# Moving four weight sums and one seventh product in the late schedule of a fused attention and feed-forward kernel

## The chip, the cores and the metric

The kernel runs on one core of a Trainium2 chip. A core has a matrix engine (TensorE, PE in the profile, with weight loads shown apart as PEld), a vector engine (VectorE, DVE), a scalar engine (ScalarE, ACT), a general engine (GpSimd, POOL) and a queue for transfers (SyncE, SP). The metric is the device time of one execution in microseconds. Four executions of the kernel before took 423.79, 424.94, 425.1 and 426.74 us; the median is 425.02 us.

## What is computed

Eight batches of twelve heads with 448 tokens and 64 columns per head go through an attention with normalised queries and keys. The result, 3584 tokens by 768 columns, goes through two weight matrices with a leaky rectifier between them.

```python
q_n, k_n = (rmsnorm(q, g_q), rmsnorm(k, g_k))
scores = scale * np.matmul(q_n, k_n.transpose(0, 1, 3, 2))
attn = softmax(scores)                    # over the last axis
x = (attn @ v), heads side by side        # 3584 x 768
h = x @ w_in                              # 768 x 2048
g = np.maximum(0.01 * h, h)
out = g @ w_out                           # 2048 x 768
```

The softmax and the last lines are abridged; inputs and output are float32.

## The kernel before

**Units.** Attention runs in units `u` of four heads: three units to a batch, 24 in all (`NU`). In each unit the loop over `d` = 0 to 3 issues the scores of one key step (`d` = 0) or two (`STEPS`), then the exponentials (`ex`, line 214) on ACT. With `d` = 0 come three more things: the shift of the exponent for this unit (`shift_max` and `shift_mm`: a maximum, a product `dg`, two small matmuls on PE at line 244, a maximum, and a small operation, four on DVE), and for the unit before it the product with the values (`pv_slot`, line 341) and the sums of the exponentials (`zcol`, line 283). After the shift, ACT copies the old unit's product (`x32`, line 295) before it computes the new exponential; DVE adds up the sums (line 300); ACT makes the reciprocals through logarithm and exponential (lines 305 and 306); SP spreads them by DMA (`rz`) and POOL multiplies (line 321).

**The queue of feed-forward work.** `push(b)` puts the feed-forward items of batch `b` into a queue, and `fill(u, d, jobs)` issues some after each group of scores, by a running account of the items' costs (1.13, 0.575 and 1.31). After each item it issues one of the step's `jobs` (normalisation of a later unit, weight sums and the like). An item is a group of matmuls on PE. What follows it on DVE and ACT is put on a list (`later`), and issued when the next item begins (`flush`). Every engine works through its instructions in the order in which they were issued.

**The late batches.** The last two batches, 6 and 7, use Strassen's scheme (seven products instead of eight) for the first weight matrix. An item is written `(n, s)`: product `n` of strip `s`, where a strip is two of the eight blocks of 128 columns in each half of the 2048. A product is six matmuls of 128x224 (line 565). In batch 6 only strips 2 and 3 are done in this way: its list is `LATE_HALF`, and an "M" in it is one plain block with six matmuls of 128x448 (`moe1`, line 363). Eight M items cover strips 0 and 1. In batch 7 all four strips are (`LATE_ALL`). Batch 6 is pushed at unit 21, `d` = 3, and issued in units 22 and 23; batch 7 follows after the last unit.

In `late1` the products work like this:

- `(1, s)` fills a bank and is copied to `u`; `(2, s)` is added to `u`, and ACT turns that into one quarter of the strip's output (line 575).
- `(7, s)` fills a second bank and is copied to `v` (line 613).
- `(6, s)` accumulates onto the bank of `(1, s)`; an addition (line 578) writes that plus `v` into the bank of `(7, s)`.
- `(5, s)` accumulates further onto the first bank; an addition puts that plus `v` into `v`, and ACT activates it.
- `(4, s)` accumulates onto the second bank, and `(3, s)` onto the first; ACT activates each from its bank.

So `(5, s)` may only start when the addition of `(6, s)` has read the bank, and `(3, s)` only after the addition of `(5, s)`. Four banks serve all of this: `hold` takes them, and `drop` puts one back at the end of a list, from whose head the next is taken. M items draw from the same list.

**Weight sums.** Four products need sums of weight blocks: `win_sum(n, x)` with `n` = 1 to 4 (line 534), each one DVE operation over 128x1536. `x` = 1 serves strips 2 and 3, and is needed by batch 6; `x` = 0 serves strips 0 and 1, which only batch 7 needs. Sum 3 is written over a block of the weights themselves, which the M items read. The four sums with `x` = 0 are jobs of unit 23: two at `d` = 0 and two at `d` = 2.

**After the late products** of batch 6 come the output items: `moe2` (line 404), in four parts for one tile, then `seven` (line 445) for two more tiles. The first part reads blocks 0 to 7 of `gt`, the activated values; the sums `s1` to `s4` of `gt` (lines 426 to 435) are made on DVE behind the four parts. `zsum_slot`, `zinv` and `xmul` finish unit 23, and then batch 7's items run to the end.

Of the kernel before, what the change touches and what calls it, by code (L numbers as in the profile page):

```python
# [18 lines left out]
def kernel(  # L19
# [18 lines left out]
    NU = B * NQ  # L38
# [7 lines left out]
    raws = ctx.enter_context(tc.tile_pool(name="raws", bufs=3))  # L46
    prep_p = ctx.enter_context(tc.tile_pool(name="prep", bufs=2))
# [75 lines left out]
    def load_v(u):  # L123
# [8 lines left out]
        n16=([P, 2, NS, 2, D], FP16, 1), qkT=([P, 2, NS, P], FP16, 3))  # L132
# [226 lines left out]
    def moe1(b, ft):  # L359
        xt = xts[b]  # L360
        hps = aux([P, 512], FP32, "hps")
        for kt in range(KT):
            nc.tensor.matmul(hps[:, 0:S], win16[:, kt // 2, kt % 2, ts(ft, P)], xt[:, kt // 2, kt % 2],  # L363
                             start=(kt == 0), stop=(kt == KT - 1))
        prelu(b, gt[:, ft, 64 * (b % 2):64 * (b % 2) + S], hps[:, 0:S])
        drop(hps)
# [22 lines left out]
    def flush():  # L389
        while pend:  # L390
            pend.pop(0)()
# [45 lines left out]
    def later(fn, *args):  # L437
        pend.append(lambda: fn(*args))
# [81 lines left out]
    def win_b(i, j, f0, n):  # L520
        c = DF // 2 * i + P * f0
        return win_f[:, HK * j:HK * j + HK, c:c + P * n]

    def win_sum(n, x, tile_=None, eng=nc.vector):
        if tile_ is None:
            ws[n, x] = win_b(1, 0, 4 * x, 4)
        else:
            pool, tag, bufs = tile_
            ws[n, x] = pool.tile([P, HK, 512], FP16, tag=tag, bufs=bufs, name="ws")
        a, b = {1: (lambda: (win_b(1, 0, 4 * x, 4), win_b(1, 1, 4 * x, 4))),  # L530
                2: (lambda: (ws[1, x], win_b(0, 0, 4 * x, 4))),
                3: (lambda: (win_b(0, 0, 4 * x, 4), win_b(1, 0, 4 * x, 4))),
                4: (lambda: (win_b(0, 1, 4 * x, 4), ws[2, x]))}[n]()
        eng.tensor_tensor(ws[n, x], a, b, op=ALU.add if n == 1 else ALU.subtract)
# [18 lines left out]
    def late1(b, tail, after):  # L553
# [45 lines left out]
        def item(n, s):  # L599
# [29 lines left out]
            for fn in after.get((n, s), ()):  # L629
# [3 lines left out]

    LATE_ALL = ((1, 0), (2, 0), (7, 0), (1, 1), (6, 0), (7, 1), (1, 2), (5, 0), (4, 0), (6, 1), (3, 0), (2, 1), (7, 2), (5, 1),
                (4, 1), (6, 2), (3, 1), (1, 3), (7, 3), (5, 2), (4, 2), (6, 3), (3, 2), (2, 2), (5, 3), (4, 3), (2, 3), (3, 3))
    LATE_HALF = ("M", "M", "M", "M", "M", "M", (1, 2), (2, 2), (7, 2), "M", (6, 2), "M", (5, 2), (4, 2), (1, 3), (3, 2), (2, 3), (7, 3),
                 (6, 3), (5, 3), (4, 3), (3, 3))

    queue = []

    def also(fn, *more):
        def both():
            fn()
            for m in more:
                m()
        return both

    def push(b):
        pair, odd = divmod(b, 2)
        fast = b > 0  # L650
        order = [f // 2 + HF * (f % 2) for f in range(FT)] if odd else range(FT)
        items = [(1.13, lambda ft=ft: (flush(), moe1(b, ft))) for ft in order]
        half = [(slice(0, 4)), (slice(4, 8))]
        late = b >= LATE
        after = {}
        if late:
            if odd:
                tt = (3, 4)
                for ns, f in (((1, 3), s1), ((4, 2), s2), ((3, 2), s3), ((5, 3), s4)):
                    after[ns] = [lambda f=f: f(tt, half[0])]  # L660
                after[3, 3] = [lambda f=f: f(tt, half[1]) for f in (s1, s2)]
            item = late1(b, odd, after)
            fts = [0, 8, 1, 9, 2, 10, 3, 11]
            items = []
            for w in (LATE_ALL if odd else LATE_HALF):
                if w == "M":
                    items.append((1.13, lambda ft=fts.pop(0): (flush(), moe1(b, ft))))
                else:
                    items.append((0.575, lambda w=w: item(*w)))
        if odd:  # L670
            tt, tn = (3, 4), (5, 6)
            items += [(1.31, fn) for fn in seven(pair, tt, tn)]
            for n, x, fs in ((len(items) - 7, 1, (s3, s4)),) if late else ((8, 0, (s1, s2)), (10, 0, (s3, s4)), (FT - 1, 1, (s1, s2)), (FT, 1, (s3, s4))):
                c, fn = items[n]
                items[n] = (c, also(fn, *[lambda f=f, x=x: later(f, tt, half[x]) for f in fs]))
            items += [(1.31, fn) for fn in seven(pair, tn, None, b == B - 1)]
        else:
            tiles = (2,) if fast else (0, 1, 2)
            std = [lambda t=t, h=h, p=p: moe2(pair, t, h, p) for t in tiles for h in range(2) for p in range(2)]
            if fast:  # L680
                tt = (0, 1)
                std[0] = also(std[0], lambda: later(s1, tt))
                std[1] = also(std[1], lambda: later(s2, tt))
                std[2] = also(std[2], lambda: later(s3, tt), lambda: later(s4, tt))
                std += seven(pair, tt)
            items += [(1.31, fn) for fn in std]
        queue.extend(items)
# [53 lines left out]
    with tc.manual_schedule():  # L741
# [182 lines left out]
        for u in range(3, NU):  # L924
            for d in range(4):
                if d > 0 or u > 3:
                    qk(u, STEPS[d])
                    if d == 0:
                        shift_max(u)
                        if narrow(u - 1):  # L930
                            pv_slot(u - 1)
                            zcol(u - 1)
                            shift_mm(u)
                            pv_out(u - 1)
                            zcol_sum(u - 1)
                        else:
                            zsum_slot(u - 1)
                            pv(u - 1)
                            shift_mm(u)
                            zinv(u - 1)  # L940
                    ex(u)
                jobs = []

                def job(fn, *args):
                    jobs.append(lambda: fn(*args))

                if d == 0:
                    if u == 3:
                        prep_norm(4)
                        gate(4)  # L950
                    elif narrow(u - 1):
                        job(zcol_inv, u - 1)
                    else:
                        xmul(u - 1)
                    if u + 4 < NU:
                        job(load, u + 4)
                    if u + 3 < NU:
                        load_v(u + 3)
                    if u < 6:
                        prep_sqp(u + 3)  # L960
                if d == 1 and narrow(u - 1) and not 5 <= u < 8:
                    xmul_pool(u - 1)
                if fed(u, d) and u > 3:
                    push(u // NQ - 1)
                if (u, d) in ((3, 1), (4, 0)):
                    for ti in range(2):
                        prep_tr(u + 1, ti, VV)
                if d == 1 and 5 <= u < NU - 1:
                    job(prep_g, u + 1)
                if u + 2 < NU:  # L970
                    if d == 1:
                        for ti in range(2):
                            job(prep_ssq, u + 2, ALL, (ti,))
                    if d == 2:
                        job(prep_rinv, u + 2)
                        for ti in range(2):
                            job(prep_norm, u + 2, ALL, (ti,))
                        if u > 3:
                            job(prep_trd, u + 2)
                if d == 1 and 4 <= u < 8:  # L980
                    job(weight_sum, u - 4, 0)
                if d == 0 and 5 <= u < 9:
                    job(weight_sum, u - 5, 1)
                if d == 2 and 5 <= u < 8:
                    job(xmul_sb, u - 1)
                if u == NU - 2 and d == 0:
                    for n, tile_ in ((1, (raws, "rq", 3)), (2, (raws, "rk", 3)), (3, None), (4, (prep_p, "sq", 3))):
                        job(win_sum, n, 1, tile_)
                    for n in (3, 1, 2, 4):
                        job(x_sum, LATE, n)  # L990
                if u == NU - 1 and d in (0, 2):
                    for n, tile_ in (((1, (raws, "rq", 3)), (3, None)), ((2, (raws, "rk", 3)), (4, (prep_p, "n16", 1))))[d // 2]:
                        job(win_sum, n, 0, tile_)
                if d == 3 and 6 <= u < NU - 3:
                    for ti in range(2):
                        job(prep_sq, u + 3, ALL, (ti,))
                fill(u, d, jobs)
# [39 lines left out]
```

## Time and profile before

| | |
|---|---|
| median of four executions | 425.02 us (423.79 to 426.74) |
| profiled execution, time | 425.1 us |
| profiled execution, span from first to last instruction | 423.3 us |
| mean granted clock of TensorE | 0.996 of full speed |
| PE busy | 404.4 us, 96% of the span |
| ACT busy | 305.0 us, 72% |
| DVE busy | 280.0 us, 66% |
| POOL busy | 83.4 us, 20% |

Line numbers (L565 and the like) are those of the kernel before. "Busy" on PE includes matmuls that run at a reduced clock. The row of granted clock gives the clock in 40 equal slices of 10.6 us, in tenths, 9 being 90% or more. In a timeline, a row is a run of like instructions: start, duration of the whole run, engine, line, operation, what is written and read, shapes, how many, and in brackets how long the engine was idle before it and what released it. Matmuls overlap, so the time that one group takes from PE is read from start to start.

The last 80 us of the span hold the stages that the change touches: unit 22 begins near 337 us, unit 23 near 356 us, batch 7's products run from 384 to 400 us, and its output items from there to the end.

### The profile page before, as it was taken

The page shows a single profiled execution, that of the slowest core. Times are in us where ns is not written, and L with a number is a line of the kernel's source. Part 1 is how long each engine was busy: PE and PEld are TensorE (multiplying, and loading weights), DVE is VectorE, ACT ScalarE, POOL GpSimd, SP SyncE. Part 2 cuts the span into 40 slices and gives each one's busy share as a digit, 9 for nine tenths or more (in the row PEclk, how much of TensorE's full clock was granted, in tenths as well). Part 3 has the DMA queues.
Part 4 walks back from the last instruction along what each step waited for, and adds up shares of the span by engine and source line. Part 5 has one row for each costly group of instructions (what it writes and reads, how often), then busy time and mean ns, then how long its engine had stood idle before and what let it go on. Part 6 is the DMA issues. An engine that isn't in the chain of part 4 may idle for free.

```text
span 423.3 us, 9152 instructions
## 1 busy us (share of the span) xinstructions
PE 404.4 (96%) x3731; PEld 218.6 (52%) x3731; DVE 280.0 (66%) x459; ACT 305.0 (72%) x474; POOL 83.4 (20%) x75
## 2 busy tenths in 40 slices
PE   7787999989999999999999999999999999899996
PEld 7454454444445544454445544454445556458953
DVE  5888685888569736675458736576459775547762
ACT  5999877768887599877887689877887576553600
POOL 1867432200010220210210210210220110200000
PEclk9999999999999999999999999999999999899999
DMA  8999997888664996678564895677532650212023
GB/s 269 218 248 243 242 251 116 210 152 201 157 152 83 205 255 93 155 182 173 145 149 82 218 210 117 161 182 170 154 67 45 132 149 2 45 39 75 2 52 98
DMA packets 71950, 62.39 MB, mean 147 GB/s; under 512 B 36325, under 2 KB 67045, under 8 KB 71909
## 3 DMA queue, kind: packets, MB, share of 16 engines
q1 hardware_dynamic: 61312, 49.62, 46.5%
q0 software_dynamic: 10272, 11.80, 17.6%
q8 instruction: 29, 0.48, 0.5%
q10 hardware_dynamic: 324, 0.39, 0.3%
q14 instruction: 13, 0.10, 0.1%
HBM read 45.61 MB, written 11.01 MB: 134 GB/s over the span
## 4 chain that ended last, share of the span: by engine, by line
PE 83%; DVE 8%; ACT 7%; issue 1%; DVEq 0%
PE hps L363 27%; PE sT L195 8%; PE sT L341 6%; PE ma L445 5%; PE md L445 5%; PE mc L445 5%; PE bank L565 5%; PE bank L445 5%; ACT et L214 5%; PE zc L283 3%; PE op L404 3%; PE mb L445 3%; DVE n L167 2%; PE warm L739 2%; PE sT L445 2%; PE bank L404 1%
## 5 line engine op out<-in xcount | busy, mean ns | idle before, releaser
L214 ACT ACTIVATE et<-sT,eb 128x896 f16<-128x896 f32 x166 | 159.6, 1010 | 18.4 <-PE sT L195 16.7
L363 PE MATMUL hps<-xt,win 128*128 128x448 f16 x600 | 121.0, 353 | 0.4 <-DVE xt L350 0.2
L363 PEld LDWEIGHTS <-win 128*128 128x128 f16 x612 | 56.8, 98 | 58.5 <-issue 10.0
L321 POOL TENSOR_TENSOR xt<-x,rz 128x896 f16<-128x896 f32 x16 | 33.7, 2107 | 143.8 <-DMA rz<-zs 96.9
L167 DVE TENSOR_TENSOR n<-rq,rinv 128x896 f16<-128x896 f32 (+2 forms) x25 | 26.7, 1072 | 51.6 <-ACT rinv L161 48.5
L357 ACT ACTIVATE gt<-hps 128x448 f16<-128x448 f32 x100 | 52.4, 549 | 5.6 <-PE hps L363 5.3
L195 PE MATMUL sT<-qkT 64*64 64x448 f16 x664 | 52.2, 363 | 4.4 <-ACT et L214 3.0
L155 DVE TENSOR_REDUCE ssq<-sq 128x14 f32<-128x896 f32 (+2 forms) x49 | 50.4, 1059 | 0.6 <-ACT sq L144 0.6
L445 PEld LDWEIGHTS <-sa 128*128 128x128 f16 x352 | 32.8, 98 | 26.3 <-issue 6.1
L295 ACT COPY x<-sT 128x896 f32<-128x896 f32 x19 | 17.2, 906 | 36.6 <-DVE sT L245 36.6
L124 POOL DMA_DIRECT2D vt<-in_v_dram x24 | 18.2, 759 | 115.5 <-PE sT L341 108.0
L195 PEld LDWEIGHTS <-qkT 64*64 64x64 f16 x672 | 15.4, 104 | 37.7 <-issue 34.2
L445 PEld LDWEIGHTS <-gt 128*128 128x128 f16 x264 | 25.2, 98 | 18.7 <-issue 2.1
L341 PE MATMUL sT<-et,vt 64*64 64x448 f16 x532 | 28.5, 349 | 0.3
L404 PE MATMUL op<-wout,gt 128*128 128x384 f16 x160 | 28.4, 327 | 0.0
L232 DVE TENSOR_REDUCE sT<-sT 128x1 f32<-128x896 f32 x22 | 24.1, 1094 | 4.9 <-PE sT L195 4.7
L341 PEld LDWEIGHTS <-vt 64*64 64x64 f16 x672 | 20.7, 107 | 11.3 <-issue 1.7
L167 DVE TENSOR_TENSOR n<-rk,rinv 128x896 f16<-128x896 f32 (+2 forms) x26 | 26.1, 1011 | 0.0
L404 PEld LDWEIGHTS <-gt 128*128 128x128 f16 x192 | 17.8, 98 | 13.8 <-issue 3.1
L445 PE MATMUL ma<-wout,gt 128*128 128x384 f16 x128 | 23.5, 326 | 0.0
L426 DVE TENSOR_TENSOR sa<-gt 128x512 f16<-128x512 f16 (+1 forms) x15 | 8.1, 543 | 15.9 <-ACT gt L357 12.1
L144 ACT ACTIVATE sq<-rq 128x896 f32<-128x896 f32 (+2 forms) x18 | 16.3, 913 | 1.3 <-DMA rq<-in_q_dram 1.3
(136 smaller groups left out, 525.5 us busy)
## 6 DMA issues: line engine op xcount, KB each, us to landing
rq<-in_q_dram SPq DMA_DIRECT2D x24, 448.0 KB, 4.4
rk<-in_k_dram SPq DMA_DIRECT2D x24, 448.0 KB, 5.6
out_dram<-ost SPq DMA_DIRECT2D x52, 192.0 KB, 2.9
rz<-zs SPq DMA_DIRECT2D x76, 112.0 KB, 2.3
vt<-in_v_dram POOLq DMA_DIRECT2D x24, 224.0 KB, 5.7
win<-in_moe_w_in_dram POOLq DMA_DIRECT2D x8, 384.0 KB, 14.2
wout<-in_moe_w_out_dram POOLq DMA_DIRECT2D x2, 1536.0 KB, 28.9
out_dram<-ost SPq DMA_DIRECT2D x4, 96.0 KB, 2.1
```

Of the source, the lines that this page charges most:

```text
L155: nc.vector.tensor_reduce(buf(u, "ssq")[:, ti, :, c[0]:c[1]], buf(u, f"sq{ti}")[:, :, c[0]:c[1]], axis=AXL.X, op=ALU.add)
L167: nc.vector.tensor_tensor(buf(u, "n16")[:, ti, c[0]:c[1]].rearrange("p s a d -> p a s d"), src[:, :, c[0]:c[1]], buf(u, "rinv")[:, ti, :, ...
L195: nc.tensor.matmul(banks[a][64 * r:64 * r + 64, 0:S].rearrange("p (t x) -> p t x", t=NS), kT(u, r, a, t), qT(u, r, a), start=True, stop=True)
L214: nc.scalar.activation(s["et"][:, t], sT[:, :, 0:S], AF.Exp, bias=s["eb"], scale=1.0)
L232: nc.vector.tensor_reduce(s["spare"][:, 511:512], sT[:, :, 0:S], axis=AXL.XY, op=ALU.max)
L321: eng.tensor_tensor(xts[b][:, g], s["x32"], s["rz"], op=ALU.mult)
L341: nc.tensor.matmul(s["pv"][r][64 * a:64 * a + 64, 0:S], vts[u % NV][64 * r:64 * r + 64, a, t], s["et"][64 * r:64 * r + 64, t, a], start=(t ...
L357: nc.scalar.activation(dst, src, AF.Prelu, bias=0.0, scale=1.0, alpha=0.01)
L363: nc.tensor.matmul(hps[:, 0:S], win16[:, kt // 2, kt % 2, ts(ft, P)], xt[:, kt // 2, kt % 2], start=(kt == 0), stop=(kt == KT - 1))
L404: nc.tensor.matmul(op2[:, 0:HC], gt[:, ft, ds(col(t), P)], wout16[:, ft, ds(HC * half, HC)], start=(ft == 0), stop=(ft == FT - 1))
L445: nc.tensor.matmul(bank[:, 0:HC], a[:, f], b[:, f], start=(first and f == 0), stop=(f == HF - 1), skip_group_check=not first)
L565: nc.tensor.matmul(bank[:, HX * i:HX * i + HX].rearrange("p (t x) -> p t x", t=NS), w, x[:, kt], start=start, stop=(kt == HK - 1), skip_gr ...
```

## The change

Three things are edited. The list `LATE_HALF` gets a new order: `(6, 3)`, the last of the sixth products, moves ahead of four items so that it and its predecessors are issued before unit 23's scores; one M moves behind it; `(1, 3)` and `(7, 3)` move forward. The two lines that made the four sums with `x` = 0 into jobs of unit 23 are removed. Instead, sums 1, 2 and 4 are put behind the DVE work of `(7, 2)`, `(6, 2)` and `(5, 2)` of batch 6, through the `after` table that `late1` already had; and sum 3 goes behind `s1`, after the first `moe2` part. `push` is called with `late` true for batch 6, so that `* late` keeps that last entry for this batch alone.

```diff
-    LATE_HALF = ("M", "M", "M", "M", "M", "M", (1, 2), (2, 2), (7, 2), "M", (6, 2), "M", (5, 2), (4, 2), (1, 3), (3, 2), (2, 3), (7, 3),
-                 (6, 3), (5, 3), (4, 3), (3, 3))
+    LATE_HALF = ("M", "M", "M", "M", "M", (1, 2), (2, 2), (7, 2), "M", (6, 2), (1, 3), "M", (5, 2), (4, 2), (7, 3), (3, 2), (2, 3),
+                 (6, 3), "M", (5, 3), (4, 3), (3, 3))
...
                 after[3, 3] = [lambda f=f: f(tt, half[1]) for f in (s1, s2)]
+            else:
+                after[7, 2] = [lambda: win_sum(1, 0, (raws, "rq", 3))]
+                after[6, 2] = [lambda: win_sum(2, 0, (raws, "rk", 3))]
+                after[5, 2] = [lambda: win_sum(4, 0, (prep_p, "n16", 1))]
...
-                std[0] = also(std[0], lambda: later(s1, tt))
+                std[0] = also(std[0], lambda: later(s1, tt), *[lambda: later(win_sum, 3, 0)] * late)
...
-                if u == NU - 1 and d in (0, 2):
-                    for n, tile_ in (((1, (raws, "rq", 3)), (3, None)), ((2, (raws, "rk", 3)), (4, (prep_p, "n16", 1))))[d // 2]:
-                        job(win_sum, n, 0, tile_)
```

No instruction is added or taken away; PE, DVE, ACT, POOL and SP have as many as before. As issued, unit 22 now runs the items M, (1,2), (2,2), (7,2) | M, (6,2), (1,3), M | (5,2), (4,2), (7,3), (3,2), (2,3), (6,3), with a bar where scores come between; before, it was M, M, (1,2) | (2,2), (7,2), M, (6,2), M | (5,2), (4,2), (1,3), (3,2), (2,3). After unit 23's first scores and its shift it runs M, (5,3), (4,3), (3,3), and before it was (7,3), (6,3), (5,3), (4,3), (3,3). The banks of the two M items around (1,3) become one and the same, and (2,3) takes the bank that (4,2) gives back.

## The prediction

> **What bounds the kernel now.** I read the page's busy shares first: TensorE (PE) is busy 96% of the span, so a gain has to come out of PE's gaps, or out of stretches in which PE runs slowly. The row of granted clock in the 40 slices and PE's list of waits name one place for each:
>
> ```profile
> PEclk9999999999999999999999999999999999899999
> ...
> PE bank L565 <- DVE bank L578: 2.0, 1, 2.0
> ```
>
> The digit below 9 is slice 35 (359.8 to 370.4 us). The one long wait late in the kernel is PE for an addition of VectorE (DVE). PE's timeline shows that these are one event (start, duration, engine, line, operation, tiles, and in brackets the idle time before it and its releaser):
>
> ```profile
> 358.50 0.74 PE L565 MATMUL bank<-xs,win 128*128 128x224 f16 x6
> 359.08 0.74 PE L565 MATMUL bank<-xs,ws 128*128 128x224 f16 x6
> 361.86 1.28 PE L565 MATMUL bank<-xs,ws 128*128 128x224 f16 x6 [2.04 <-DVE bank L578]
> 362.94 1.33 PE L565 MATMUL bank<-xs,win 128*128 128x224 f16 x6
> 364.06 1.33 PE L565 MATMUL bank<-xt,ws 128*128 128x224 f16 x6
> 365.18 1.53 PE L404 MATMUL bank<-wout,gt 128*128 128x384 f16 x8
> ```
>
> These are (7,3), (6,3), (5,3), (4,3), (3,3) and the first output part. One product takes 0.58 us from start to start (358.50 to 359.08). (5,3) starts 2.78 us after (6,3), so **2.20 us** are lost. The next three take 365.18 - 361.86 = 3.32 us instead of 3 x 0.575 = 1.73: **1.60 us** more, and the output part some 0.07. The table by stretch (PE, weight load, DVE, ACT, POOL busy; then granted clock, DMA share, GB/s) gives the reason:
>
> ```profile
> 360.00:361.00 1.00, 0.00 (x0) 0.00 (x0) 1.00 (x2) 1.00 (x3) 0.00 (x0) 1.00 0.00 0
> 361.00:362.00 1.00, 0.14 (x1) 0.10 (x1) 1.00 (x3) 0.58 (x2) 0.00 (x0) 0.95 0.00 0
> 362.00:363.00 1.00, 1.00 (x7) 0.82 (x6) 0.67 (x1) 0.00 (x0) 0.00 (x0) 0.50 0.09 24
> ...
> 364.00:365.00 1.00, 1.00 (x8) 0.79 (x7) 0.00 (x0) 0.85 (x2) 0.00 (x0) 0.50 0.76 169
> ```
>
> After the gap the granted clock is 0.50, until about 365.3. The place costs 2.20 + 1.60 + 0.07 = **3.87 us**. DVE's timeline shows what (5,3) waits for:
>
> ```profile
> 359.79 0.61 DVE L613 COPY v<-bank 128x448 f32<-128x448 f32 x1
> 360.32 0.95 DVE L534 TENSOR_TENSOR ws<-win 128x1536 f16<-128x1536 f16 x1
> 361.19 0.62 DVE L578 TENSOR_TENSOR bank<-bank,v 128x448 f32<-128x448 f32 x1
> ```
>
> The addition of (6,3) stands behind the weight sum (0.87 us, start to start), and that behind (7,3)'s copy, which had to wait for the four DVE operations of the last scores' shift and for the denominators' sum.
>
> **What the change removes.** In its order (7,3) and (6,3) are issued before the last scores, and their copy and addition stand ahead of the shift on DVE. After the shift come a full item "M", then (5,3), (4,3), (3,3). The 2.20 us gap goes, and with it what made the clock fall: -3.87. PE's work is the same, only reordered.
>
> **What the weight sums cost.** Four of 0.87 us, in new places. After (7,2): (1,2), (2,2), (7,2) now start at 346.12, 346.70 and 347.27, DVE works through their copy, addition and copy to 348.8, and the sum ends at 349.7; the next addition, of (6,2), is ready at 350.3. After (6,2): 351.0 to 351.9; (5,2)'s addition comes at 353.7. After (5,2): 354.3 to 355.2; (7,3)'s copy is next, and the shift's maximum, queued behind two more additions, starts at 357.7 and its product dg ends at 359.1, with PE at the shift's matmul at 359.45. In the output stage, behind s1: ends near 366.2, before the first output half (about 367.0) is to be copied. Each is covered by 0.3 us or more; without cover it would cost its 0.87. In the old place the sums at 372.34 and 373.32 delayed nothing on PE, so nothing is won there.
>
> **What is late next.** The order moves ScalarE (ACT) work too, and its queue is in program order. Durations are ACT's own rows:
>
> ```profile
> 348.37 1.91 ACT L214 ACTIVATE et<-sT,eb 128x896 f16<-128x896 f32 x2 [0.36 <-PE sT L195]
> ...
> 359.10 0.91 ACT L295 COPY x<-sT 128x896 f32<-128x896 f32 x1 [1.68 <-DVE sT L245]
> 359.90 1.01 ACT L214 ACTIVATE et<-sT,eb 128x896 f16<-128x896 f32 x1
> 360.80 0.39 ACT L305 ACTIVATE zs<-zs 128x224 f32<-128x224 f32 x1
> 361.22 0.39 ACT L306 ACTIVATE zs<-zs 128x224 f32<-128x224 f32 x1
> ```
>
> (a) The M items before and after (1,3) use the same bank, so the second waits for the first's activation. That stands behind (2,2)'s output activation (348.3, 0.48 to the next start) and two exponentials of 0.90: it runs 350.60 to 351.15. PE is there at 350.72: **0.47** idle.
> (b) (2,3) takes the bank of (4,2), free after that item's activation. ACT does the second M's activation (352.5), two exponentials (352.96 to 354.75), (5,2)'s output (0.46), then (4,2)'s, ending at 355.74. PE is there at 355.22: **0.56**.
> (c) (3,3) needs (5,3)'s addition with only (4,3) in between: 0.74 to (5,3)'s last result, 0.04, 0.62, 0.04 make 1.44 after its start, against 2 x 0.575: **0.30**. At half clock, in the old trace, this was hidden.
> (d) The first output part's seventh weight load reads what (2,3) and (3,3) activate. From the shift's matmul, ACT needs 0.66, then copy 0.80, exponential 0.90, the late M 0.42, logarithm 0.43, exponential 0.30, and three outputs 0.46, 0.46, 0.53: 4.96 us. PE is there after 0.06 + 1.13 + 2 x 0.575 + 0.30 + 0.575 + 0.98 = 4.19: **0.81** with the release.
>
> Together 2.14 us. Each lies between nothing (its producer earlier than I place it) and about twice itself (if DVE is also late); the order and durations are known, so I take the values. Sum: -3.87 + 2.14 = **-1.73 us**. The scores that start at 366.64 now should start near 364.9. From there the order is the old one with banks renamed. The last unit but one has its reciprocals 1.4 us later (363.0 instead of 361.6), so SP's four issues of rz and POOL's product (366.1 to 368.6) move to about 370; the first x sum of the last batch asks at 382.66, near 381 then. Covered by 10 us. SP's stores and POOL keep their order.
>
> [...] By the row it cost 1.67 more, and the row decides: -1.73. [...] The profiled execution, which did, took 425.1 against a median of 425.02, so I take it as typical; 423.79, the fastest of the four, may be one without.
>
> Do my own waits lower the clock? Nearest row: from 8.96 to 12.0 us PE was idle for 1.02 and 0.82 us and the clock stayed 1.00. My densest pair (c, d) idles 1.1 in 2.7 us. I take no loss.
>
> **The rivals.**
> 1. The waits (a) to (d) are smaller, down to none, since each is a difference of two chains. Up to 3.87 gained: 421.2; half of them: 422.3. For it: PE waits seldom on ACT elsewhere late in the trace. Against: ACT's queue is in order and these banks are taken by name.
> 2. The slow clock is not typical of the old kernel: -2.20 + 2.14, so 425.0. For it: [...] a spread of 3 us over four runs. Against: the profiled run lies on the median.
> 3. The scattered waits bring the half clock themselves. The mechanism is a, b, c, d spread over about 14 us[...]. One leaves 425.1, two give 425.1 - 1.73 + 3.4 = 426.8, three 428.5. It decides once two stretches are below 1.00. Against it: 8.96 to 12.0 above.
> 4. The sums delay single additions after all, so the gap only moves: 425.1 to 426.
>
> **The numbers.** The profiled execution took 425.1 us with a span of 423.3; 1.8 lies around the span and stays. 425.1 - 1.73 = **423.4**; its own range is 422.6 to 424.2. Chances: forecast 0.50, rival 1 0.20, rivals 2 and 4 0.18, rival 3 0.12. The range, 421.5 to 425.8, leaves out two in ten. What a measurement can tell is about 0.5%, 2.1 us, so the forecast lies just inside "same": rival 1 and somewhat under half of the forecast's spread are faster (0.42), the most of rival 3 is slower (0.10), 0.48 stays.
>
> **What would show it.** Right: no DVE wait of 2 us at L565; granted clock 1.00 from 340 on; PE waits on ACT of about 0.5, 0.6 and 0.8 us in this stretch; the scores after the first output part near 364.9. Wrong: half clock anywhere in 345 to 368 (rival 3), hardly any ACT wait (rival 1), an addition L578 that starts right after a sum L534 with PE idle (rival 4), or repeats of the old kernel at clock 1.00 (rival 2).

## The result, and the profile after

| | before | changed |
|---|---|---|
| median | 425.14 us (55 executions) | 423.75 us (34 executions) |
| ratio to before, 95% interval | | 0.9969 [0.9961, 0.9978], 1.3 us less (0.9 to 1.7) |
| measured again (experiment 7) | | 0.9963 [0.9952, 0.9974], 1.6 us less (1.1 to 2.0) |
| profiled execution: time, span | 425.1, 423.3 us | 424.08, 422.3 us |

The gain is clear of the noise, and at 0.3 to 0.4% smaller than the 0.5% that the prediction took for the least that a measurement can tell. The two profiled spans differ by 1.0 us only. PE's timeline of the changed kernel shows the stretch in question:

```profile
345.18 0.57 PE L195 MATMUL sT<-qkT 64*64 64x448 f16 x8
...
350.87 0.74 PE L565 MATMUL bank<-xt,win 128*128 128x224 f16 x6
351.91 1.29 PE L363 MATMUL bank<-xt,win 128*128 128x448 f16 x6 [0.30 <-ACT gt L357]
...
355.38 0.74 PE L565 MATMUL bank<-xt,ws 128*128 128x224 f16 x6
356.54 0.73 PE L565 MATMUL bank<-xt,win 128*128 128x224 f16 x6 [0.42 <-ACT gt L575]
...
361.97 0.74 PE L565 MATMUL bank<-xs,win 128*128 128x224 f16 x6
362.85 0.73 PE L565 MATMUL bank<-xt,ws 128*128 128x224 f16 x6
363.42 1.14 PE L404 MATMUL bank<-wout,gt 128*128 128x384 f16 x6
365.19 0.50 PE L404 MATMUL bank<-wout,gt 128*128 128x384 f16 x2 [0.62 <-ACT gt L575]
365.62 0.57 PE L195 MATMUL sT<-qkT 64*64 64x448 f16 x8
```

The first and the last line are the scores of unit 22's second step and those after the first output part, and the distance between them is the measure used from here on: **the stretch**. It is 365.62 - 345.18 = 20.44 us. The same two rows of the kernel before:

```profile
344.48 0.57 PE L195 MATMUL sT<-qkT 64*64 64x448 f16 x8
...
366.64 0.57 PE L195 MATMUL sT<-qkT 64*64 64x448 f16 x8
```

Before, the stretch was thus 366.64 - 344.48 = 22.16 us. The one wait of 2 us is gone and four small ones have come, all where the old kernel had none. (The idle time in brackets is less than what is lost, since matmuls overlap; from start to start the four cost 0.47, 0.58, 0.30 and 0.79 us.) The table by stretch shows full clock on both sides of the largest one:

```profile
363.00:364.00 1.00, 1.00 (x10) 0.81 (x9) 0.00 (x0) 0.97 (x4) 0.00 (x0) 1.00 0.09 16
364.00:365.00 1.00, 0.56 (x4) 0.11 (x2) 0.00 (x0) 1.00 (x3) 0.00 (x0) 1.00 0.00 0
365.00:366.00 1.00, 0.81 (x10) 0.26 (x10) 0.83 (x2) 0.13 (x1) 0.00 (x0) 1.00 0.56 115
```

PE works 0.56 us in the middle row, ACT works throughout, and the clock (third number from the right) stays 1.00.

So the stretch gave 1.72 us. Where did the spans lose 0.70 of it again? In the first 20 us, which the change does not touch. The page's row of granted clock and one row of the table by stretch:

```profile
PEclk9699999999999999999999999999999999999999
```

```profile
14.00:15.00 1.00, 1.00 (x10) 0.48 (x9) 1.00 (x2) 0.97 (x3) 1.00 (x2) 0.50 1.12 164
```

This execution ran at half clock from about 11.1 to 17.9 us, where the profiled execution of the kernel before had full clock. The two are 0.07 us apart at the first matmul after 11.9 us (12.03 and 11.96) and 0.70 us at the scores after the half clock (18.17 and 17.47), and 0.70 us they stay until 345.18 and 344.48. So 6.8 us at half clock took only 0.70 us of time here, since PE has idle time there (in the kernel before it is busy 0.74 us of the row shown, here all of it). After the stretch the two take the same: 423.3 - 366.64 = 56.66 and 422.3 - 365.62 = 56.68 us. Sum: +0.70 - 1.72 + 0.02 = -1.00 us.

### The profile page after: what moved, and what is told of

Its sections match the earlier page's. It is cut to its first block, busy times and chain, and to the rows that moved or that the text cites. A ratio compares the mean times of both kernels' runs of the same rounds, so it can differ in the third digit from the quotient of the medians.

```text
span 422.3 us, 9149 instructions
## 1 busy us (share of the span) xinstructions
PE 404.5 (96%) x3731; PEld 217.3 (51%) x3731; DVE 282.7 (67%) x459; ACT 304.7 (72%) x474; POOL 83.4 (20%) x75
## 4 chain that ended last, share of the span: by engine, by line
PE 77%; DVE 10%; ACT 8%; DMA 2%; issue 2%; SPq 0%; DVEq 0%; ACTq 0%
PE hps L363 25%; PE sT L195 8%; PE sT L341 5%; PE ma L445 5%; PE mc L445 5%; ACT et L214 5%; PE bank L445 5%; PE md L445 5%; PE op L404 3%; PE bank L565 3%; PE zc L283 3%; PE mb L445 3%; DVE n L167 2%; PE sT L445 2%; PE bank L404 1%
## 5 line engine op out<-in xcount | busy, mean ns | idle before, releaser
L214 ACT ACTIVATE et<-sT,eb 128x896 f16<-128x896 f32 x166 | 159.6, 1010 | 17.9 <-PE sT L195 16.1
L363 PE MATMUL hps<-xt,win 128*128 128x448 f16 x594 | 119.8, 353 | 0.4 <-DVE xt L350 0.2
L357 ACT ACTIVATE gt<-hps 128x448 f16<-128x448 f32 x99 | 51.9, 549 | 5.5 <-PE hps L363 5.3
L195 PE MATMUL sT<-qkT 64*64 64x448 f16 x664 | 53.1, 368 | 2.9 <-ACT et L214 1.8
```

The costliest lines, as they stand in the source:

```text
L195: nc.tensor.matmul(banks[a][64 * r:64 * r + 64, 0:S].rearrange("p (t x) -> p t x", t=NS), kT(u, r, a, t), qT(u, r, a), start=True, stop=True)
L214: nc.scalar.activation(s["et"][:, t], sT[:, :, 0:S], AF.Exp, bias=s["eb"], scale=1.0)
L357: nc.scalar.activation(dst, src, AF.Prelu, bias=0.0, scale=1.0, alpha=0.01)
```

## The experiments

The theory after the result: before, the stretch lost 3.87 us, of which 2.20 were the wait of (5,3) and 1.67 the half clock that followed; the changed kernel loses 2.14 us in waits on ACT and DVE. What is to be told apart: list order against the place of the sums, wait against clock, and whether the new waits are ACT's queue and the banks. The table gives each kernel's stretch in its own trace and the ratio of its times to those of the kernel before, measured beside it.

| kernel | stretch | median | ratio, 95% interval |
|---|---|---|---|
| before | 22.16 | | 1 |
| changed | 20.44 | 423.75 | 0.9969 [0.9961, 0.9978] |
| 1 list order alone | 20.43 | 424.99 | 0.9991 [0.9981, 1.0001] |
| 2 sums alone | 20.13 | 423.6 | 0.9959 [0.9944, 0.9975] |
| 3 before, gap filled | 20.80 | 424.04 | 0.9974 [0.9964, 0.9983] |
| 4 changed, late reciprocals | 19.75 | 423.15 | 0.9949 [0.9934, 0.9965] |
| 5 as 4, third list order | 18.69 | 421.75 | 0.9906 [0.9888, 0.9923] |
| 6 as 1, multiplication on DVE | 20.43 | 423.94 | 0.9956 [0.9938, 0.9973] |

**1. The list order alone.** The new `LATE_HALF` in the kernel before; the sums stay jobs of unit 23.

> The new list order alone; the four weight sums stay jobs of unit 23, as before. Theory (the order takes (6,3)'s addition out of the gap, and with the gap the half clock): sum 1 now stands ahead of (5,3)'s addition, so (3,3) starts about 0.4 us later than in the changed kernel, but ScalarE's queue is later still at the first output part, so that this is absorbed: as the changed kernel, 423.7 us within 0.4, granted clock 1.00 from 340 us on. Rival (the place of the sums is what counts): back to the kernel before, about 425.1.

The stretch came out as in the changed kernel (365.07 - 344.64 = 20.43 us), with full clock (a mean of 1.000 over the profiled execution). But the time gained almost nothing: the theory missed, and the rival's number was right, for a cause that neither had named. PE's timeline shows the loss eight microseconds later, at the third product of the output stage:

```profile
344.64 0.57 PE L195 MATMUL sT<-qkT 64*64 64x448 f16 x8
...
365.07 0.57 PE L195 MATMUL sT<-qkT 64*64 64x448 f16 x8
...
372.79 0.57 PE L195 MATMUL sT<-qkT 64*64 64x448 f16 x8
374.18 1.46 PE L445 MATMUL bank<-wout,gt 128*128 128x384 f16 x8 [0.82 <-DVE ost L461]
```

DVE's timeline gives the reason, and GpSimd's (POOL) timeline the reason for that:

```profile
368.16 0.69 DVE L432 TENSOR_TENSOR sa<-gt 128x1024 f16<-128x1024 f16 x1
368.76 2.57 DVE L435 TENSOR_TENSOR sa<-gt,sa 128x1024 f16<-128x1024 f16 x1
371.26 0.54 DVE L408 COPY ost<-bank 128x384 f32<-128x384 f32 x1
371.73 0.94 DVE L534 TENSOR_TENSOR ws<-ws,win 128x1536 f16<-128x1536 f16 x1
372.70 0.96 DVE L534 TENSOR_TENSOR ws<-win,ws 128x1536 f16<-128x1536 f16 x1
373.58 0.55 DVE L461 COPY ost<-bank 128x384 f32<-128x384 f32 x1
```

```profile
368.46 2.32 POOL L321 TENSOR_TENSOR xt<-x,rz 128x896 f16<-128x896 f32 x1 [18.38 <-DMA rz<-zs]
```

The sum s4, which takes 0.69 us like s3 before it, takes 2.57 here and ends (371.33) shortly after POOL's multiplication does (370.78). The copy at L461, which PE's next product waits for, then stands behind two weight sums (0.97 and 0.88 us, start to start). Neither delay alone reaches PE: in the changed kernel s4 takes 2.57 us too, and without the sums PE does not wait; experiment 6 has the sums without the long s4. So the new order needs the sums moved: it brings POOL's multiplication onto s4, and the sums must not stand behind that.

**2. The sums alone.** The changed kernel with the old `LATE_HALF`.

> The old list order with the weight sums in their new places. Theory: (6,3)'s addition no longer stands behind sum 1, so the gap ahead of (5,3) shrinks from 2.20 to about 1.36 us; that is too little to bring the half clock; (3,3) then waits 0.30 at full clock. 425.1 - 0.84 - 1.67 + 0.30 = about 422.9, faster than the changed kernel, since none of its waits on ScalarE arise. Rival 1 (a gap of 1.4 us is enough for the half clock): about 424.3. Rival 2 (the half clock was not typical of the kernel before): 424.6.

The stretch is 364.88 - 344.75 = 20.13 us, 2.03 less than before. The wait is 361.47 - 359.36 - 0.575 = 1.54 us (1.36 was expected), and the clock stays at 1.00 from 359 to 364 us:

```profile
359.36 0.74 PE L565 MATMUL bank<-xs,ws 128*128 128x224 f16 x6
361.47 0.73 PE L565 MATMUL bank<-xs,ws 128*128 128x224 f16 x6 [1.37 <-DVE bank L578]
362.04 0.74 PE L565 MATMUL bank<-xs,win 128*128 128x224 f16 x6
362.92 0.73 PE L565 MATMUL bank<-xt,ws 128*128 128x224 f16 x6
```

The products take 0.57 us again after the gap, and (3,3) has its 0.31 us. In this trace, taking one weight sum of 0.87 us out of the gap was enough for the whole effect of the clock. The time of 423.6 us misses the expected 422.9, but cannot be told from the changed kernel's; the stretch is 0.31 us shorter. So the sums need no new order: moved alone, they gain as much as the whole change.

**3. The gap filled.** The kernel before, with matmuls that nobody reads:

```diff
             elif n == 5:
+                if s == 3 and not tail:
+                    warm(30, held[0][0])
                 mm(g[1, s], 5, s, xs[1], False)
```

> The kernel before, with 30 small matmuls of ones into a free bank issued between (6,3) and (5,3), some 1.7 us of work that nobody reads, so that the wait of (5,3) stays but the matrix engine is busy in it. Theory (1.67 us of the place are half clock, 2.20 wait): granted clock 1.00 after the gap, (3,3) waits 0.30, time 425.1 - 1.37 = about 423.8. Rival (the half clock is not typical of the kernel before, the wait alone counts): unchanged, 425.1.

PE's timeline with the added work (L741):

```profile
358.68 0.74 PE L565 MATMUL bank<-xs,ws 128*128 128x224 f16 x6
359.26 1.84 PE L741 MATMUL bank<-onesp 128*128 128x128 f16 x30
361.46 0.73 PE L565 MATMUL bank<-xs,ws 128*128 128x224 f16 x6 [0.36 <-DVE bank L578]
362.03 0.74 PE L565 MATMUL bank<-xs,win 128*128 128x224 f16 x6
```

(5,3) waits as long as ever (361.46 - 358.68 - 0.575 = 2.20 us), but what follows runs at full clock (1.00 from 358 to 364 us), and the stretch is 20.80 us: 1.36 less, as expected (1.67 of clock, and 0.30 given back at (3,3)). The time falls by 1.1 us (0.7 to 1.5). This shows the share of the clock by itself; and since a kernel that never paid it would have gained nothing, it shows that most executions of the kernel before did.

**4. The reciprocals later.** In the changed kernel, `zcol_inv` of unit 22 is issued one step later:

```diff
-                    elif narrow(u - 1):
+                    elif narrow(u - 1) and u < NU - 1:
                         job(zcol_inv, u - 1)
+                    elif narrow(u - 1):
+                        pass
...
+                if d == 1 and u == NU - 1:
+                    zcol_inv(u - 1)
```

> The changed kernel, with the logarithm and exponential of unit 22's denominators (and the DMAs after them) issued one group of scores later in unit 23, behind the two exponentials there. Theory (the wait of the first output part is ScalarE's queue, 0.73 us of it these two): that wait falls from 0.79 to about 0.1 us, time 423.75 - 0.7 = about 423.05. Rival (that wait is set by the additions on VectorE, or the multiplication on GpSimd, now 5 us later, is late for the last batch): unchanged or slower, 423.7 or more.

The stretch is 19.75 us, 0.69 less, and the output part runs through but for 0.10 us. ACT's timeline: the outputs (L575) follow the late M's activation (L357) directly, and the two short operations come after the next exponentials:

```profile
361.77 0.55 ACT L357 ACTIVATE gt<-bank 128x448 f16<-128x448 f32 x1
362.20 0.59 ACT L575 ACTIVATE gt<-v 128x448 f16<-128x448 f32 x1
362.66 0.99 ACT L575 ACTIVATE gt<-bank 128x448 f16<-128x448 f32 x2
364.57 1.91 ACT L214 ACTIVATE et<-sT,eb 128x896 f16<-128x896 f32 x2 [0.92 <-PE sT L195]
366.37 0.39 ACT L305 ACTIVATE zs<-zs 128x224 f32<-128x224 f32 x1
```

So the wait ahead of the last two matmuls of the output part was ACT's queue. The time of 423.15 us agrees.

**5. A third list order,** on top of the late reciprocals:

```diff
+    LATE_HALF = ("M", "M", "M", "M", "M", "M", (1, 2), (2, 2), (7, 2), "M", (6, 2), (1, 3), (5, 2), (4, 2), (7, 3), (3, 2), (6, 3),
+                 (2, 3), "M", (5, 3), (4, 3), (3, 3))
```

> The changed kernel with the late reciprocals of the run before and a third list order: six M items first, then (1,2), (2,2), (7,2), M, (6,2), (1,3), (5,2), (4,2), (7,3), (3,2), (6,3), (2,3), M, (5,3), (4,3), (3,3). No two M items around (1,3) share a bank any more, and (2,3) comes one product later. Theory (the waits of 0.47 and 0.58 us on ScalarE are those two banks): both go, 0.30 at (3,3) and about 0.1 at the output part stay; 423.15 - 1.0 = about 422.1. Rival (the two exponentials ahead of each activation are late whatever bank is taken, so the waits move to another product): 423.1.

```profile
344.33 0.57 PE L195 MATMUL sT<-qkT 64*64 64x448 f16 x8
...
363.02 0.57 PE L195 MATMUL sT<-qkT 64*64 64x448 f16 x8
```

The stretch is 363.02 - 344.33 = 18.69 us, and the waits of 0.47 and 0.58 us for those two banks are gone; 0.30 us at (3,3) and 0.09 at the output part are left. The time is 421.75 us, 4.0 us (3.3 to 4.8) below the kernel before on the same chip. The trace accounts for 3.47 us; the rest is within the interval. Experiment 7 sets it beside the changed kernel.

**6. The multiplication moved,** to tell the two causes in experiment 1 apart:

```diff
+                if u == NU - 1 and d == 3:
+                    job(xmul_sb, u - 1)
-                if d == 1 and narrow(u - 1) and not 5 <= u < 8:
+                if d == 1 and narrow(u - 1) and not 5 <= u < 8 and u < NU - 1:
                     xmul_pool(u - 1)
```

> The list order alone, as in the first run, but with unit 22's multiplication done by VectorE late in unit 23 instead of by GpSimd. In the first run the sum s4 took 2.57 us while GpSimd multiplied, and later the first product of the output stage waited 0.82 us for its copy behind s4 and two weight sums. Theory (the two engines collide): s4 is back to about 0.7 us, the wait of 0.82 is gone, 425.0 - 0.85 = about 424.15. Rival (the two weight sums alone are the cause): the wait stays, 425.0, or more by VectorE's own 1.1 us.

s4 is back to 0.68 us, the copy at L461 starts at 373.08, and the third product at 373.74 without a wait:

```profile
369.21 0.68 DVE L435 TENSOR_TENSOR sa<-gt,sa 128x1024 f16<-128x1024 f16 x1
...
373.08 0.55 DVE L461 COPY ost<-bank 128x384 f32<-128x384 f32 x1
```

The ratio fell from 0.9991 to 0.9956, more than the 0.85 us of the wait; the two were measured on different chips, so only the direction and the row are taken from it. So POOL's multiplication beside it was the cause of the late s4: 2.57 us with it, 0.68 without.

**7. Both once more on one chip.** The changed kernel, then the third list order.

> The changed kernel once more, beside the third list order on the same chip. Theory (the changed kernel is 1.73 us faster than the kernel before in an execution with the late half clock, and 0.06 in one without): mean granted clock over the executions about 0.003 above that of the kernel before, gain between 1.0 and 1.7 us.

> The third list order with late reciprocals once more. Theory: its traces differ from the changed kernel's by 1.75 us in the stretch, so it should be about 1.75 us faster than the changed kernel on the same chip. Rival (the 421.75 us of its first run, 2.0 below the changed kernel, was in part that chip's start): 1 us or less.

The changed kernel took 423.59 us against 425.1, ratio 0.9963 [0.9952, 0.9974]. The third order took 422.05 us, ratio 0.9932 [0.9908, 0.9956], and its stretch was 363.71 - 345.02 = 18.69 us again. The difference of the two medians is 1.54 us, near the 1.75 of the traces, though with six executions of the one it is not sharp. So the third order is faster than both kernels. Averaged over the executions, the granted clock was 0.9957 for the changed kernel and 0.9931 for the kernel before, 0.0026 apart, where 0.003 was expected.

## Why the prediction was right

**The old loss, 3.87 us.** Right for an execution with the late half clock, and shown in parts: experiment 3 keeps the wait of 2.20 and removes the clock's part alone. One reading in it is off: the four operations of the shift were over at 359.20, before the last result of (7,3) at 359.24 (358.50 + 0.74), and only the denominators' sum still stood ahead of its copy.

**What removes it.** The prediction gave the gain to the new order and held the sums to be a cost that has to be covered. The order does close the gap, but experiment 2 shows that it was not needed: with the sums moved alone, a shorter gap stays, the clock stays up, and the time is as low. The order alone gained at most 0.8 us (experiment 1). In the forecast's own sum the closed gap and the new waits cancel (2.20 against 2.14) and the gain is the clock's 1.67 us; that the sums alone keep the clock as well, the prediction did not see.

**The new waits, 2.14 us.** Predicted 0.47, 0.56, 0.30 and 0.81; measured 0.47, 0.58, 0.30 and 0.79. They were worked out from rows of the old trace and the order of issue alone. Experiment 4 shows the last to be ACT's queue, and experiment 5 that the first two were the banks.

**The stretch, -1.73 us.** Measured -1.72 in the traces. The scores were predicted at 364.9; they came at 365.62 in an execution that was 0.70 late since its start.

**The time, 423.4 us.** Measured 423.75. The gain over the executions was 1.3 us, not 1.7, and the term that was too large is the half clock taken as typical of every execution. A sign that the prediction had named for rival 2 did appear: of the 82 executions of the kernel before that were timed beside the experiments, 11 have a mean granted clock of 1.000, with the same order of issue. One stretch of 3.4 us at half clock makes that 0.996, as in the profiled execution of the kernel before, so they had none. Among those of experiment 7, six of the kernel before at 1.000 have a median of 423.9 us and six of the changed kernel at 1.000 have 423.3: without the half clock some 0.6 us were left to gain, roughly, with so few.

How many executions had the late half clock can only be estimated. Experiment 3 gained 1.1 of the 1.36 us of its trace, which makes about 0.8 of them. In experiment 7 the mean clocks differ by 0.0026 of 423 us, 1.1 us of lost clock, and one stretch of half clock, 3.4 us long, loses 1.7: about 0.65. This takes the stretches at the start to be alike in both kernels. With 0.7 of the executions at 1.72 us and the rest at 0.36 (next paragraph), the gain is 1.3 us, as measured.

**Rival 2's sum** was wrong by a term: without the half clock, (3,3) waits 0.30 in the old kernel as well, so the old loss is then 2.50 and not 2.20, and 0.36 us remain to be gained. Experiment 3's stretch (20.80 against 20.44) shows that difference.

**The sums at 372 and 373 us, "nothing is won there".** Wrong for the new order, as experiment 1 shows: left there, they cost PE 0.82 us of idle time. The step looked at the old order only, in which POOL multiplied at 366.1, ahead of s2. The prediction had seen that POOL moves to about 370 and had checked who waits for POOL, but not which DVE operation would run beside it.

**Cover for the sums.** For the first it did not hold on DVE: behind (7,2) the sum took 1.97 us instead of 0.95, and the addition of (6,2) began at 351.36, 0.3 us after its product was done, where the prediction had 0.6 us in hand. It cost nothing, because PE needs this addition only for (5,2), at 353.64. The prediction had not seen that POOL multiplies at that time (last section).

**What the row decided.** The row of granted clock decided rightly: the gap of 2.20 us cost 1.67 us of clock in the trace, and by the estimate above it did so in most executions (experiment 3 gained 1.1 us with the gap kept). Rival 3 did not appear: no granted clock below 1.00 between 340 and 418 us in either trace of the changed kernel.

## What to carry to other kernels

When a gap on the matrix engine is closed, look for the clock behind it: here the smaller part of a wait (one operation of 0.87 us ahead in another engine's queue) carried the whole half clock with it (1.67 us), and moving it would have been enough. When work is reordered, count again what stands ahead of each release in its engine's queue, by name of the buffer (here two short operations on ACT were worth 0.69 us), and then ask which pairs of operations on different engines now fall together (s4 took 2.57 us instead of 0.68). An operation that delays nothing in the old order may be what delays the new one, as the weight sums at 372 and 373 us did here, by 0.82 us.

## What was not expected of the hardware

**GpSimd and VectorE held each other up.** In the changed kernel's DVE and POOL timelines:

```profile
349.47 1.97 DVE L534 TENSOR_TENSOR ws<-win 128x1536 f16<-128x1536 f16 x1
351.36 0.62 DVE L578 TENSOR_TENSOR bank<-bank,v 128x448 f32<-128x448 f32 x1
...
369.31 2.57 DVE L435 TENSOR_TENSOR sa<-gt,sa 128x1024 f16<-128x1024 f16 x1
```

```profile
348.53 2.09 POOL L321 TENSOR_TENSOR xt<-x,rz 128x896 f16<-128x896 f32 x1 [14.56 <-DMA rz<-zs]
368.78 2.55 POOL L321 TENSOR_TENSOR xt<-x,rz 128x896 f16<-128x896 f32 x1 [18.16 <-DMA rz<-zs]
```

The weight sum, 0.95 us elsewhere, began while POOL multiplied and ended 0.82 us after POOL did (350.62). s4, 0.68 us elsewhere, took 2.57 and ended 0.55 us after a multiplication that ended at 371.33. In experiment 2, where POOL multiplied from 367.19 to 369.27, it was s2 that took 2.44 us, from 367.37 to 369.81, and s3 and s4 their 0.68. Each thus ended after POOL by a little less than the time that it takes alone. POOL took longer too where it began during such a sum: 2.55 us here and 2.32 in experiment 1, both begun during s3, against 2.08 in experiment 2. In the changed kernel an addition and a copy out of a bank, at 348.40 and 348.94, kept their 0.62 and 0.61 us beside the multiplication of 2.09 us at 348.53. Experiment 6, which takes POOL's instruction away, gives s4 its 0.68 us back. Why these operations collide and those do not, the traces do not show.

**How small a gap keeps the clock.** In the traces, a wait of 2.20 us brought half clock for 3.4 us; 1.54 us in the same place did not, and neither did 1.1 us spread over 2.7. The length of the gap does not decide alone: at the start of the changed kernel's trace half clock came at 11.1 us, after idle times of 1.05 and 0.77 us that ended at 8.37 and 10.04, while in the kernel before idle times of 1.02 and 0.82 us, ended at 9.99 and 11.96, brought none. The 11 executions of the kernel before at a clock of 1.000 had the same order of issue; how long they waited was not measured. What else decides, and what a gap between 1.54 and 2.20 us brings in this place, was not tried.
